# Starting the V projection with the second tile, centred and not yet scaled

## The chip, the cores and the metric

The kernel runs on one core of a Trainium2 chip. The metric is the device time of one execution in microseconds (us). The engines are named as in the profile: PE (TensorE, matmuls), PEld (its weight loads), DVE (VectorE), ACT (ScalarE), POOL (GpSimd) and SP (SyncE, which only issues DMAs here).

## The reference, cut to what matters

There are 2048 tokens of width 576. The input is layer-normalised once, and attention and a gated feed-forward layer are added to it:

```python
xn = _layernorm(x, axis=-1)                 # (x - mean) / sqrt(var + 1e-5)
return x + _A_ref(xn, A_wqkv, A_wo) + _B_ref(xn, B_w1, B_w3, B_w2)

# A: 32 heads of width 18, a causal window of 256 tokens
qkv = (x @ wqkv).reshape(B, S, 3, H, Dh)
scores = einsum("bhqd,bhkd->bhqk", q, k) * (Dh ** -0.5)
p = softmax(where(mask, scores, -1e9))
o = einsum("bhqk,bhkd->bhqd", p, v) @ wo
# B: feed-forward width 4608
h = silu(xn @ w1) * (xn @ w3);  out = h @ w2
```

All inputs are bf16. What matters here is that a row of V is linear in the normalised row of x. The factor 1/sqrt(var + eps) belongs to a token, so it may be applied to the row of V after the matmul just as well as to the row of x ahead of it.

## The kernel before

The tokens are worked on in four chunks of 512 (`CH`), a chunk in four tiles of 128 tokens. A chunk goes through q, k and v projections, then 36 units of the feed-forward layer with attention steps dealt in between, then the second products. The change is in the **prologue**, the first 13 us or so, in which the four tiles of chunk 0 are loaded, normalised, transposed and projected to V before the q and k jobs start. Only chunk 0 has such a prologue; later chunks are prepared beside other work.

The program is written as one list of operations (`add(engine, fn, r=, w=, j=)`). Each engine carries out its own operations strictly in the order of the list; `resolve` turns the reads and writes of named buffers into semaphore waits between engines. So an operation that waits holds up all that is behind it on its engine.

A tile t of the prologue takes these steps:
- The load of x (L304; `xp`), and on POOL a copy that doubles the last 64 columns (L963), so that the 576 columns become 640, five blocks of 128.
- Mean and variance. DVE does this in three operations for tiles 0, 2 and 3 (`ln_stats`: L394 twice, L397). For tile 1 ACT does it in two passes with a running sum (`ln_stats_act`): a Copy with scale -1/D (L385), whose sum is minus the mean, and a Square with that as its bias (L388).
- The root on ACT (`ln_sqrt`, L367), the reciprocal on DVE (L372) and the normalising pass on DVE (`ln_apply`, L411), which writes `xn[t % 2]`.
- The transposes on PE (`xn_turn`, L426): ten of 64 columns for a tile, in pairs on the two halves of the array, into two PSUM banks or two pairs of them; then two moves out of PSUM into `xnT` (L439), on ACT, or one on ACT and one on DVE.
- V on PE (`proj_part`, L491): a first part of 8 matmuls and a second of 10, with 64 rows and 288 columns each. `proj_begin` issues a job's first part and then ends the job that is pending; `proj_end` only ends the pending one. Four moves per tile (`v_evac`, two on ACT L540, two on DVE L542) bring V into `va`.

Some filler matmuls (`warm`, `warm_halves`, L902 and L908) stand in the waits ahead of V. The moves of V can be held back in lists (`moves`, `late`) and put into the program later, so that they don't stand ahead of the next tile's transposes on ACT and DVE.

`xnT` has two slots, one for the chunk at work and one for the next chunk. In the prologue slot 1 is empty. The q and k jobs (L491 with 512 columns) read all four tiles of slot 0, and weights `wp` that POOL copies into order (`deal_...`, L946) as soon as the loads of wqk land. `xn_swap` (L454) sends slot 0 with its halves exchanged to `xnS`, which the feed-forward units (L759) read from their fifth matmul pair on. SP's queue issues, in this order: wv, wqk, the first feed-forward weights (`load_w13`, L328, which wait for the tile named in `behind`), then `xn_swap`.

PSUM has eight banks: three job pairs, `JOBS`, of which `job()` takes one after the other, and the pair `SC`, which the transposes use and V of the last tile.

Of the kernel before, what the change touches and what calls it, by code (L numbers as in the profile page):

```python
# [5 lines left out]
dt = mybir.dt  # L6
# [158 lines left out]
def bass_parallel_sum__sliding_block__glu_gated_swiglu__prompt_kernel(  # L165
# [32 lines left out]
    with ExitStack() as es:  # L198

        def sb(name, shape, dtype=dt.bfloat16):  # L200
            return es.enter_context(nc.sbuf_tensor(name, shape, dtype))
# [12 lines left out]
        eps = sb("eps", [128, 1], dt.float32)  # L214
        sd = [sb(f"sd{i}", [128, 1], dt.float32) for i in range(2)]
        xnT = sb("xnT", [128, 2, 5, CH])
        xnS = sb("xnS", [128, 4, CH])
# [162 lines left out]

        def ln_stats_act(t, s, between):
# [3 lines left out]
            add("act", lambda e: e.activation(junk, xp[s][:, 0:D], ACT.Copy, scale=-1.0 / D, accum_out=vpe[i][:]),  # L385
                r=[("xp", s)], w=[("vpe", i), *keys])
            between()
            add("act", lambda e: e.activation(junk, xp[s][:, 0:D], ACT.Square, bias=vpe[i][:], scale=1.0, accum_out=mv[i][:, 1:2]),  # L388
                r=[("xp", s), ("vpe", i)], w=[("mv", i), *keys])
# [24 lines left out]

        def xn_turn(t, pairs, eng, between=(), by_rows=False):
            i = t % 2
            c, tt = divmod(t, TB)
            ranges = ((0, 2), (2, 5))
            for n, (k0, k1) in enumerate(ranges):
                for k in range(k0, k1):  # L420
                    for r in range(2):
                        r0 = 64 * r
                        b = pairs[n][r]
                        bv = half_bank(b)[:, 64 * k:64 * k + 64]
                        new = k == k0 and (n == 0 or pairs[0] != pairs[1])
                        add("pe", lambda e, bv=bv, r0=r0, k=k: e.transpose(  # L426
                            bv, xn[i][r0:r0 + 64, k * 128:(k + 1) * 128], ident[r0:r0 + 64, r0:r0 + 64],
                            tile_position=(r0, 0)),
                            r=[("xn" if k < 4 else "xnd", i), "ident"], **{"w" if new else "j": [("ps", b)]})
            for what in between:  # L430
                what()
            dst = xnT[:, c % 2, :, tt * 128:(tt + 1) * 128].rearrange("p k (r f) -> p k r f", f=64)
            for n, (k0, k1) in enumerate(ranges):
                b = pairs[n][0]
# [4 lines left out]
                move = (lambda e, d=d, s=s: e.tensor_copy(d, s)) if eng[n] == "dve" else (lambda e, d=d, s=s: e.activation(d, s, ACT.Copy))  # L439
                add(eng[n], move, r=[("ps", b) for b in pairs[n]],  # L440
                    **({"j": [("xnT", c % 2, tt), ("xnTb", tt)] + [("xnTa", tt)] * by_rows} if n else
                       {"w": [("xnT", c % 2, tt), ("xnTa", tt), ("xnTb", tt)]}))

# [22 lines left out]
        def proj_part(c, what, banks, part, behind=()):  # L466

            kind, i = what
            last = []
            early = kind == "v" and c == 0  # L470
            order = range(4 + part if kind == "v" else 5 - part)
            for n in order:
                for r in range(2):
# [4 lines left out]
                    if kind == "q":  # L478
                        t = pair_of(c, i)[x]
                        st, mv = wp[rows, kd, t, :], xnT[rows, c % 2, kd, :]  # L480
                        keys = [("wpd" if n == 4 else "wp", t)] + xk(c)
                    elif kind == "8":
                        out_ = PS[:, banks[x], 0:CH // 2]
                        st, mv = wp[rows, kd, i, :], xnT[rows, c % 2, kd, x * (CH // 2):(x + 1) * (CH // 2)]
                        keys = [("wpd" if n == 4 else "wp", i)] + xk(c)
                    else:
                        out_ = PS[:, banks[x], 0:HD]
                        st, mv = xnT[rows, c % 2, kd, i * 128:(i + 1) * 128], wv[rows, kd, x * HD:(x + 1) * HD]
                        keys = ["wvd" if kd == 4 else "wv", (("xnTb" if kd // 2 else "xnTa"), i) if early and kd < 4 else ("xnT", c % 2, i)]
                    first = part == 0 and n == 0  # L490
# [43 lines left out]
        def v_evac(c, tt, b, r, eng, p):  # L534
# [3 lines left out]
            kw = {"j" if p else "w": [("va", pos)]}  # L538
            if eng == "act":
                add("act", lambda e, dst=dst, src=src: e.activation(dst, src, ACT.Copy), r=[("ps", b), ("ps", b + 1)], **kw)  # L540
            else:
                add("dve", lambda e, dst=dst, src=src: e.tensor_copy(dst, src), r=[("ps", b), ("ps", b + 1)], **kw)  # L542
# [413 lines left out]
        def deal_last(h, d, lo, hi):  # L956
            s0 = lo - (lo > SPREAD)
            deal(h, d, [8], lambda o: o[:, :, 8, s0 * Dh // 2:(s0 + hi - lo) * Dh // 2].rearrange("p k (g c) -> p k g c", c=Dh // 2),
                 lambda i: i[:, :, 1, lo:hi, 3 * Dh // 2:2 * Dh])

        for t in range(TB):
            end = xp[xslot[t]][:, 512:640].bitcast(dt.float32)
            add("pool", lambda e, end=end: e.tensor_copy(end[:, 32:64], end[:, 0:32]), r=[("xp", xslot[t])], w=[("xpd", xslot[t])])  # L963

        moves, late = [], []
# [349 lines left out]
```

## Time and profile before

| what | us |
|---|---|
| median of three runs | 554.58 |
| the three runs | 554.48, 554.58, 555.00 |
| the profiled execution, its own time | 554.48 |
| its span from first to last instruction | 552.7 |
| mean granted TensorE clock | 1.00 |

In a row of the timeline the first number is the start and the second the length, both in us from the start of the span; then come the engine, the line of the kernel, the operation, the tiles written and read, the shapes and a count. Brackets tell how long the engine had been idle and what ended that. A row with a count joins several neighbours. In a row of an answer by line the three numbers are the shortest, median and longest duration in ns. In a row of groups they are the total in us and the mean in ns.

### The profile page before, as it was taken

What the parts mean: (1) busy time and instruction counts of PE and PEld (TensorE: products, weight loads), DVE (VectorE), ACT (ScalarE), POOL (GpSimd) and SP (SyncE); (2) the same over time, 40 slices, a digit from 0 to 9 for tenths busy, and PEclk for the clock granted to TensorE, in tenths of its full rate; (3) what the DMA queues carried; (4) which work ended last, traced back from release to release, by engine and by line L of the source; (5) the groups of instructions that cost most, each with busy time, mean ns of one, the idle gap of its engine ahead of it and who ended that gap; (6) DMA issues with size and microseconds to landing.
All of it is one profiled execution on the core that took longest, in us unless ns stands there. A gap on an engine that the chain in (4) does not pass through costs nothing.

```text
span 552.7 us, 18355 instructions
## 1 busy us (share of the span) xinstructions
PE 548.7 (99%) x8071; PEld 338.7 (61%) x8071; DVE 313.7 (57%) x584; ACT 258.8 (47%) x360; POOL 212.3 (38%) x388
## 2 busy tenths in 40 slices
PE   8999999999999999999999999999999999999998
PEld 5555544777555544577765554559886555445776
DVE  8466797710468886651056988665105567866311
ACT  6456776000288567700047857760005784775000
POOL 6324675400047465530005656643001553663100
PEclk9999999999999999999999999999999999999999
DMA  9997899676577953758646875466763673541750
GB/s 253 209 199 167 197 221 202 138 200 182 141 144 145 177 135 102 176 143 208 182 111 140 172 146 146 112 155 167 194 179 87 138 173 102 152 110 52 195 152 23
DMA packets 128038, 86.00 MB, mean 156 GB/s; under 512 B 35702, under 2 KB 125646, under 8 KB 127958
## 3 DMA queue, kind: packets, MB, share of 16 engines
q1 hardware_dynamic: 89138, 62.80, 49.7%
q10 hardware_dynamic: 38820, 22.02, 15.7%
q8 instruction: 63, 1.03, 0.8%
q14 instruction: 17, 0.14, 0.1%
HBM read 71.29 MB, written 2.36 MB: 133 GB/s over the span
## 4 chain that ended last, share of the span: by engine, by line
PE 98%; DMA 1%; ACT 0%; DVE 0%; issue 0%
PE ps L759 51%; PE ps L832 29%; PE ps L491 10%; PE ps L621 6%; PE ps L689 3%; DMA xp<-in_A_x_dram 1%; DVE stats L394 0%; ACT hT L388 0%; ACT sd L367 0%; PE ps L426 0%; ACT xnT L439 0%; DVE ofin L854 0%; DVE mv L397 0%
## 5 line engine op out<-in xcount | busy, mean ns | idle before, releaser
L759 PE MATMUL ps<-xnT,w 64*128 64x512 bf16 x1400 | 185.3, 376 | 0.0
L759 PE MATMUL ps<-xnS,w 64*128 64x512 bf16 x1120 | 150.6, 376 | 0.0
L832 PE MATMUL ps<-w,hT 64*128 64x288 bf16 x2292 | 144.0, 282 | 0.0
L774 DVE SCALAR_TENSOR_TENSOR gs<-th,ps 128x512 bf16<-128x512 bf16 x144 | 97.9, 680 | 77.7 <-ACT th L768 77.2
L832 PEld LDWEIGHTS ps<-w,hT 64*128 64x128 bf16 x2292 | 117.1, 94 | 24.8 <-issue 0.2
L768 ACT ACTIVATE th<-ps 128x512 bf16<-128x512 f32 x144 | 85.7, 595 | 60.5 <-PE ps L759 59.3
L759 PEld LDWEIGHTS ps<-xnT,w 64*128 64x128 bf16 x1400 | 66.8, 94 | 63.7
L777 DVE SCALAR_TENSOR_TENSOR hT<-gs,ps 128x512 bf16<-128x512 bf16 x144 | 98.9, 687 | 5.0
L658 POOL TENSOR_TENSOR pt<-pt,mk 128x256 bf16<-128x256 bf16 (+1 forms) x143 | 85.6, 622 | 26.3 <-ACT pt L630 26.3
L630 ACT ACTIVATE pt<-ps 128x1024 bf16<-128x1024 f32 (+1 forms) x80 | 80.7, 1009 | 24.0 <-PE ps L621 23.3
L658 POOL TENSOR_TENSOR hT<-hT,mk 128x256 bf16<-128x256 bf16 (+1 forms) x52 | 30.3, 604 | 160.4 <-ACT hT L630 160.4
L759 PEld LDWEIGHTS ps<-xnS,w 64*128 64x128 bf16 x1120 | 53.6, 94 | 51.0
L504 ACT ACTIVATE stage<-ps 128x512 bf16<-128x512 f32 x16 | 9.6, 597 | 139.2 <-PE ps L491 139.2
L863 DVE TENSOR_TENSOR ofin<-ps,xp 128x288 bf16<-128x288 f32 x31 | 12.2, 451 | 98.2 <-PE ps L832 98.2
L621 PE MATMUL ps<-qv,kv 64*128 64x320 bf16 (+4 forms) x528 | 51.4, 260 | 0.0
L621 PEld LDWEIGHTS ps<-qv,kv 64*128 64x128 bf16 x528 | 26.2, 94 | 27.7 <-ACT pt L630 0.8
L491 PE MATMUL ps<-xnT,wp 64*128 64x512 bf16 (+1 forms) x360 | 38.4, 355 | 0.0
L722 DVE STREAM_TRANSPOSE od<-oq 128x256 bf16<-128x256 bf16 x64 | 25.4, 426 | 12.1 <-POOL oq L715 12.1
L630 ACT ACTIVATE hT<-ps 128x1024 bf16<-128x1024 f32 (+1 forms) x28 | 28.4, 1014 | 7.8 <-PE ps L621 7.6
L658 POOL TENSOR_TENSOR stage<-stage,mk 128x256 bf16<-128x256 bf16 (+1 forms) x44 | 24.9, 587 | 14.4 <-ACT stage L630 14.4
L630 ACT ACTIVATE stage<-ps 128x1024 bf16<-128x1024 f32 (+1 forms) x24 | 24.3, 1014 | 7.9 <-PE ps L621 7.8
L491 PEld LDWEIGHTS ps<-xnT,wp 64*128 64x128 bf16 x360 | 18.4, 94 | 14.3
(92 smaller groups left out, 394.2 us busy)
## 6 DMA issues: line engine op xcount, KB each, us to landing
w<-in_B_w_dram SPq DMA_DIRECT2D x210, 192.0 KB, 4.0
w<-in_B_w_dram ACTq DMA_DIRECT2D x70, 288.0 KB, 3.6
xp<-in_A_x_dram SPq DMA_DIRECT2D x29, 144.0 KB, 4.1
out_dram<-ofin SPq DMA_DIRECT2D x31, 72.0 KB, 2.0
xnS<-xnT SPq DMA_DIRECT2D x8, 256.0 KB, 5.0
oT<-od SPq DMA_DIRECT2D x56, 36.0 KB
pt<-in_A_wqkv_dram SPq DMA_DIRECT2D x4, 288.0 KB, 5.3
hT<-in_B_w_dram SPq DMA_DIRECT2D x6, 192.0 KB, 7.1
```

The lines of the kernel that those rows point to most:

```text
L491: op = add("pe", lambda e, out_=out_, st=st, mv=mv, n=n, r0=r0, first=first: e.matmul(out_, st, mv, start=first, stop=(part == 1 and n == ...
L621: add("pe", lambda e, r0=r0, out_=out_, kb=kb, q0=q0, nb=nb: e.matmul(out_, kb4[r0:r0 + 64, g, kb + NV - NB, :] if kb < 0 else kv[r0:r0 + ...
L630: add("act", lambda e: e.activation(pt_slot(sl)[:, :, 0:w], PS[:, SC[0]:SC[1] + 1, 0:w], ACT.Exp, scale=scale), r=[("ps", b) for b in SC], ...
L658: add("pool", lambda e, vb=vb, mm=mm: e.tensor_tensor(vb, vb, mm, ALU.mult), r=(key if n == 0 else []) + ["mk"], **{"w" if n == 0 else "j" ...
L689: add("pe", lambda e, p=p, q=q, pr=pr, sl=sl, g=g, pos=pos, q0=q0, nb=nb, col=col, first=first, n=n: e.matmul(PS[32 * q:32 * q + VW, banks ...
L722: add("dve", lambda e: e.transpose(od[i][:, g % 2, c0:c0 + CH // 2], oq[:, c0:c0 + CH // 2]), r=["oq", "oq0"], **{"j" if half or g % 2 els ...
L759: op = add("pe", lambda e, n=n, r0=r0, r=r, k=k, src=src: e.matmul(PS[:, b0 + r, :], wt[r0:r0 + 64, k, fl * 128:(fl + 1) * 128], src, star ...
L768: add("act", lambda e: e.activation(th[i][:], PS[:, bg, :], ACT.Tanh, scale=0.5), r=[("ps", bg)], w=[("th", i)])
L774: add("dve", lambda e: e.scalar_tensor_tensor(out=gs[i][:], in0=th[i][:], scalar=1.0, in1=PS[:, bg, :], op0=ALU.add, op1=ALU.mult), r=[("t ...
L777: add("dve", lambda e: e.scalar_tensor_tensor(out=hT[:, u, :], in0=gs[i][:], scalar=0.5, in1=PS[:, bu, :], op0=ALU.mult, op1=ALU.mult), r= ...
L832: op = add("pe", lambda e: e.matmul(PS[:, bank, 0:w], stat, move, start=new, stop=False, skip_group_check=True, **tile), r=keys, after=hel ...
L863: add("dve", lambda e: e.tensor_tensor(ofin[:, o, :], PS[:, bank, 0:HD], xp[xs[n]][:, d0:d0 + HD], ALU.add), r=[("ps", bank), ("xp", xs[n] ...
```

## The change

The second tile (tile 1, the one whose statistics ACT makes) becomes the first one that V is made of. Step by step:
- `centre`: one added pass on DVE adds minus the mean to tile 1 and writes `xn[1]`, without the scale. It stands ahead of tile 0's reciprocal.
- Tile 1 is transposed first, into slot 1 of `xnT` (banks of two job pairs), then tile 0 into slot 0 (both halves in `SC`). ACT does all four moves, with the root of tile 2 between tile 0's two moves (`halfway`).
- ACT's Square pass of tile 1 and the statistics' end come only after these moves (`ln_square_act`). Tile 1's root on ACT and its reciprocal and normalising pass on DVE are gone. In their place `root_and_scale` puts three operations on POOL: variance, power -0.5 (`rstd1`), and a 640-column pass that writes the wholly normalised tile 1 into `scaled`, which is a part of `od[0]`. They stand ahead of the `deal` copies.
- V is made in the order tile 1, tile 0, tile 2, tile 3. Tile 1's V is multiplied by `rstd1` on its way out of PSUM (a scale operand on ACT, a `tensor_scalar` on DVE).
- Tile 1 is transposed a second time, from `scaled`, between the two parts of tile 3's V, into slot 0, for the q and k jobs and the feed-forward layer. One move is on ACT, one on DVE.
- Tile 3's root stands ahead of tile 2's move on ACT. All V moves are in lists by tile and put in one by one (`move_v`).
- `proj_end` for tile 3's V comes ahead of the first q job's first part, and `xn_swap` after it in the list.
- The filler pairs are of 256, 128 and 128 columns instead of 256, 256 and 128. `load_w13` waits for tile 0's second move instead of tile 1's.

```diff
+        def centre(s):
+            add("dve", lambda e: e.tensor_scalar(xn[1][:, :], xp[s][:, :], vpe[1][:, 0:1], None, op0=ALU.add),
+                r=[("xp", s), ("xpd", s), ("vpe", 1)], w=[("xn", 1), ("xnd", 1)])
+
+        def root_and_scale(s):
+            add("pool", lambda e: e.tensor_scalar(var1[:], mv[1][:, 1:2], 1.0 / D, 1e-5, op0=ALU.mult, op1=ALU.add),
+                r=[("mv", 1)], w=["var1"])
+            add("pool", lambda e: e.tensor_tensor(rstd1[:], var1[:], neghalf[:], ALU.pow),
+                r=["var1", "neghalf"], w=["rstd1"])
+            add("pool", lambda e: e.tensor_scalar(
+                scaled[:, :], xp[s][:, :], vpe[1][:, 0:1], rstd1[:, 0:1], op0=ALU.add, op1=ALU.mult),
+                r=[("xp", s), ("xpd", s), ("vpe", 1), "rstd1"], w=[("od", 0)])
...
+            if c == 0 and tt == 1:
+                by = rstd1[64 * r:64 * r + 64, 0:1]
+                if eng == "act":
+                    fn = lambda e: e.activation(dst, src, ACT.Copy, scale=by)
+                else:
+                    fn = lambda e: e.tensor_scalar(dst, src, by, None, op0=ALU.mult)
+                add(eng, fn, r=[("ps", b), ("ps", b + 1), "rstd1"], **kw)
...
-        ln_stats_act(1, xslot[1], lambda: ln_sqrt(0))
-        ln_sqrt(1, 1.0 / D)
+        ln_mean_act(1, xslot[1])
+        ln_sqrt(0)
...
+        centre(xslot[1])
         normalise(0)
-        xn_turn(0, (SC, JOBS[1]), ("act", "act"))
-        for cols in (256, 256, 128):
-            warm_halves(JOBS[0], cols)
-        ln_stats(2, xslot[2], 0)
-        ln_stats(2, xslot[2], 1)
-        normalise(1)
-        ln_stats(2, xslot[2], 2)
-        proj_begin(0, ("v", 0))
-        ln_sqrt(2)
-        xn_turn(1, (SC, JOBS[1]), ("act", "act"))
-        load_w13([("xnTb", 1)])
+        xn_turn(1, (JOBS[0], JOBS[1]), ("act", "act"), slot=1)
+        for cols in (256, 128):
+            warm_halves(JOBS[2], cols)
+        for part in range(3):
+            ln_stats(2, xslot[2], part)
+        xn_turn(0, (SC, SC), ("act", "act"), halfway=lambda: ln_sqrt(2))
+        ln_square_act(1, xslot[1])
+        root_and_scale(xslot[1])
+        warm_halves(JOBS[2], 128)
+        proj_begin(0, ("v", 1))
+        load_w13([("xnTb", 0)])
         ln_stats(3, xslot[3], 0)
         normalise(2)
         ln_stats(3, xslot[3], 1)
         ln_stats(3, xslot[3], 2)
-        proj_end(moves, late)
-        proj_begin(0, ("v", 1))
-        ln_sqrt(3)
-        xn_turn(2, (SC, SC), ("act", "dve"), by_rows=True)
+        proj_end(*moves[1])
+        proj_begin(0, ("v", 0))
+        xn_turn(2, (SC, SC), ("act", "dve"), [lambda: ln_sqrt(3)], by_rows=True)
+        proj_end(*moves[0])
         normalise(3)
-        moves.pop(0)()
-        first = [late.pop(0)]
-        proj_end(moves, late)
         proj_begin(0, ("v", 2))
-        xn_turn(3, (SC, SC), ("act", "dve"), first, by_rows=True)
-        for move in moves + late:
-            move()
+        move_v(1, "act")
+        move_v(1, "act")
+        move_v(1, "dve")
+        xn_turn(3, (SC, SC), ("act", "dve"), by_rows=True)
+        move_v(1, "dve")
+        proj_end(*moves[2])
+        proj_begin(0, ("v", 3), SC)
+        move_v(0, "act")
+        move_v(0, "dve")
+        xn_turn(1, (JOBS[2], JOBS[2]), ("act", "dve"), by_rows=True, of=(scaled, ("od", 0), ("od", 0)))
+        for tt in (0, 2):
+            for eng in ("dve", "act"):
+                while moves[tt][eng == "act"]:
+                    move_v(tt, eng)
+        proj_end()
         xn_swap(0, ("sp", "sp"))
-        proj_end()
-        proj_begin(0, ("v", 3), SC)
```

More of the change, by code (lines that the diff above doesn't have):

```diff
@@ L386, in ln_stats_act, with ln_square_act @@
                 r=[("xp", s)], w=[("vpe", i), *keys])
-            between()
+        def ln_square_act(t, s):
+            i = t % 2
+            junk = hT[:, 0:3, :].rearrange("p t c -> p (t c)").bitcast(dt.float32)[:, 0:D]
+            keys = [("h", n) for n in range(3)]
             add("act", lambda e: e.activation(junk, xp[s][:, 0:D], ACT.Square, bias=vpe[i][:], scale=1.0, accum_out=mv[i][:, 1:2]),
@@ L468, in proj_part @@
             kind, i = what
+            vs = 1 if c == 0 and i == 1 else c % 2
             last = []
@@ L487, in proj_part @@
                         out_ = PS[:, banks[x], 0:HD]
[L488 to L489 removed]
+                        st, mv = xnT[rows, vs, kd, i * 128:(i + 1) * 128], wv[rows, kd, x * HD:(x + 1) * HD]
+                        keys = ["wvd" if kd == 4 else "wv", (("xnTb" if kd // 2 else "xnTa"), i) if early and kd < 4 else ("xnT", vs, i)]
                     first = part == 0 and n == 0
@@ L959, in deal_last, with double_end, move_v @@
                  lambda i: i[:, :, 1, lo:hi, 3 * Dh // 2:2 * Dh])
+        scaled = od[0][:, :, :].rearrange("p a q -> p (a q)")[:, 0:640]
+        def double_end(t):
+            end = xp[xslot[t]][:, 512:640].bitcast(dt.float32)
+            add("pool", lambda e: e.tensor_copy(end[:, 32:64], end[:, 0:32]), r=[("xp", xslot[t])], w=[("xpd", xslot[t])])
         for t in range(TB):
-            end = xp[xslot[t]][:, 512:640].bitcast(dt.float32)
-            add("pool", lambda e, end=end: e.tensor_copy(end[:, 32:64], end[:, 0:32]), r=[("xp", xslot[t])], w=[("xpd", xslot[t])])
-        moves, late = [], []
+            double_end(t)
+        moves = [([], []) for _ in range(TB)]
+        def move_v(tt, eng):
+            moves[tt][eng == "act"].pop(0)()
         for p in range(2):
```

21 lines of the change are left out of this document (13 added, 8 removed).

## The prediction

> **What bounds the kernel now.** I read the page's header and busy times first, then the table of windows, then the timeline of the first 13 us engine by engine, then the answers by line for the operations that the change adds.
>
> ```profile
> span 552.7 us, 18355 instructions
> ...
> PE 548.7 (99%) x8071; PEld 338.7 (61%) x8071; DVE 313.7 (57%) x584; ACT 258.8 (47%) x360; POOL 212.3 (38%) x388
> ```
> ```profile
> 6.52:550.30 543.78, 543.78 (x7998) 335.32 (x7998) 308.89 (x573) 254.92 (x352) 208.82 (x374) 1.00 0.66 155
> ```
> The second row is a window; after its length stand the busy times in the order PE, PEld, DVE, ACT, POOL, then clock, DMA share and GB/s. From the first V matmul at 6.52 to 550.30 TensorE is busy for all 543.78 us. So the change can move the time only by the place that TensorE has reached in its list at some point of the prologue; whatever it wins or loses there is carried to the end one for one. Of the 554.48 us of the profiled execution 1.78 lie outside the span and stay. The shown runs have their median at 554.58, 0.10 above it.
>
> I therefore compare one landmark: the start of the second q job (12.93), when all four V tiles and the first half of the first q job are done.
>
> ```profile
> 5.72 0.32 PE L426 MATMUL ps<-ident,xn 64*128 64x64 bf16 x10 [0.56 <-DVE xn L411]
> ...
> 6.52 0.71 PE L491 MATMUL ps<-wv,xnT 64*128 64x288 bf16 x8 [0.21 <-ACT xnT L439]
> ...
> 9.89 0.31 PE L426 MATMUL ps<-ident,xn 64*128 64x64 bf16 x10
> 10.12 1.28 PE L491 MATMUL ps<-wv,xnT 64*128 64x288 bf16 x18
> 11.24 1.25 PE L491 MATMUL ps<-xnT,wp 64*128 64x512 bf16 x10
> ...
> 12.93 1.26 PE L491 MATMUL ps<-xnT,wp 64*128 64x512 bf16 x10
> ```
> Start to start, ten transposes of one tile cost 10.12-9.89 = 0.23. Eighteen V matmuls (one tile: 8 in its first part, 10 in its second) cost 11.24-10.12 = 1.12, which is 0.50 and 0.62. The first half of the first q job and one V second part stand between 11.24 and 12.93, so that half costs 1.69-0.62 = 1.07. From the first V matmul to the landmark: 4 x 1.12 + 3 x 0.23 + 1.07 = 6.24. Before it took 12.93-6.52 = 6.41, so 0.17 is waiting.
>
> **The change, part by part.** After it there are again three sets of transposes behind the first V matmul (third tile, fourth tile, and the second tile once more, scaled), since both first tiles' are now ahead. The same 6.24 is to be done, from another start and with other waits.
>
> *Start.* The rows of ScalarE and VectorE:
>
> ```profile
> 3.77 0.69 ACT L385 ACTIVATE hT<-xp 128x576 f32<-128x576 bf16 x1 [0.21 <-DMA xp<-in_A_x_dram]
> 4.36 0.19 ACT L385 ACTIVATION_READ_ACCUMULATOR hT<-xp 128x1 f32 x1
> 4.69 0.29 ACT L367 ACTIVATE sd<-mv,eps 128x1 f32<-128x1 f32 x1
> 4.89 0.76 ACT L388 ACTIVATE hT<-xp,vpe 128x576 f32<-128x576 bf16 x1
> 5.56 0.19 ACT L388 ACTIVATION_READ_ACCUMULATOR hT<-xp,vpe 128x1 f32 x1
> ...
> 6.00 0.38 ACT L439 ACTIVATE xnT<-ps 128x256 bf16<-128x256 bf16 x1
> ...
> 6.28 0.48 ACT L439 ACTIVATE xnT<-ps 128x384 bf16<-128x384 bf16 x1
> ```
> ```profile
> 5.02 0.16 DVE L372 RECIPROCAL rstd<-sd 128x1 f32<-128x1 f32 x1 [0.36 <-ACT sd L367]
> 5.22 0.45 DVE L411 TENSOR_SCALAR xn<-xp,mv,rstd 128x640 bf16<-128x640 bf16 x1
> 5.58 0.81 DVE L394 BATCH_NORM_STATS2 stats<-xp 128x6 f32<-128x288 bf16 x2
> ```
> A handover costs 0.03 to 0.06 (5.22+0.45 = 5.67, then TensorE at 5.72). The mean of the second tile is there at 4.55; the added centring, of the shape of L411, runs 4.60 to 5.05 in the 0.36 that VectorE idles ahead of its reciprocal, so the first tile's chain (5.02, 5.22, transposes at 5.72) does not move. The second tile's transposes start at 5.10, their two moves on ScalarE at 5.38 and 5.66 (0.28 behind, 0.28 apart, as 5.72, 6.00 and 6.28), done at 5.76 and 6.14. The weights then decide:
>
> ```profile
> L894 SPq DMA_DIRECT2D wv<-in_A_wqkv_dram x2: 581/582/582, 1.7 to 2.3; - x2
> L890 SPq DMA_DIRECT2D wv<-in_A_wqkv_dram x1: 418/418/418, 1.3 to 1.3; - x1
> ...
> DMA to landing us min/median/max: 4.5/4.7/4.7
> ```
> L890 is issued at 1.3 and lands 4.5 to 4.7 later, 5.8 to 6.0; V starts at 6.03 instead of 6.52, 0.49 sooner. Its last slice (2.3 + 4.7 = 7.0 at most) is wanted at 7.03. The filler matmuls taken out (three pairs of sizes 256, 256, 128 become 256, 128, 128) stood in waits and cost nothing either way. V of the second tile: 6.03 to 7.15.
>
> *ScalarE's new order.* The first tile's moves both need all ten transposes, since they share one bank pair; the distance for that is 0.35 (9.89 to 10.24 below).
>
> ```profile
> 7.98 0.45 DVE L394 BATCH_NORM_STATS2 stats<-xp 128x6 f32<-128x288 bf16 x1
> 8.47 0.21 DVE L397 BATCH_NORM_AGGREGATE mv<-stats 128x2 f32<-128x12 f32 x1
> ```
> ```profile
> 8.71 0.30 ACT L367 ACTIVATE sd<-mv,eps 128x1 f32<-128x1 f32 x1 [0.61 <-DVE mv L397]
> 8.91 0.42 ACT L439 ACTIVATE xnT<-ps 128x320 bf16<-128x320 bf16 x1
> ...
> 10.24 0.44 ACT L439 ACTIVATE xnT<-ps 128x320 bf16<-128x320 bf16 x1 [0.62 <-PE ps L426]
> ```
> First move 6.07. The third tile's statistics end at 6.39, its aggregate at 6.64, and the root that stands between the two moves runs at 6.67; the second move starts 0.20 behind it (8.71 to 8.91), 6.87 to 7.35. That just serves V of the first tile, 7.15 to 7.65 for its first part. Behind it Square takes 7.25 to 8.01, its sum is read 7.92 to 8.11. The third tile is normalised 7.20 to 7.65 (root out at 6.97, reciprocal 7.00), transposed 7.70 to 7.93 (0.05 lost), and V of the first tile ends at 8.55.
>
> *First new wait.* The fourth tile's second statistics stand behind that normalisation: 7.56 to 8.02, aggregate 8.05 to 8.26, root at 8.29. The third tile's move on ScalarE is queued behind that root though its data are there at 8.05: 8.49 to 8.91. V of the third tile starts at 8.97 instead of 8.55: 0.42 lost. Before, the same start was 9.89-0.50 = 9.39. So the earlier start itself is worth nothing beyond this point; what counts is that this chain is 0.42 sooner.
>
> *Second new wait.* The scale of the second tile, on GpSimd:
>
> ```profile
> L376 POOL TENSOR_SCALAR vpe<-mv x12: 221/221/222, 71.2 to 317.4; 128x1 f32<-128x1 f32 x12
> ```
> ```profile
> L378 POOL TENSOR_TENSOR rstd<-vpe,neghalf x12: 567/567/572, 71.5 to 317.7; 128x1 f32<-128x1 f32 x12
> ```
> ```profile
> L540 ACT ACTIVATE va<-ps 64x288 bf16<-64x288 f32 x32 | 12.8, 401 | 4.5 <-PE ps L491 4.1
> ```
> Sum at 8.11, variance 8.15, power 0.30 behind it (71.2 to 71.5), 8.45 to 9.02. Two V moves of the second tile stand on ScalarE ahead of the fourth tile's move and wait for it until 9.05. One costs 0.40 by L540; the scale operand is not in a row of that shape, so bounds: nothing, or the 0.08 by which L388 with an operand exceeds L385 without; I take 0.08, the like instruction. [...] Moves 9.05 to 9.53 and 9.54 to 10.02. The fourth tile, transposed 9.47 to 9.70, could move at 9.82 and moves at 10.03 to 10.46. V of the third tile ends 10.32, V of the fourth starts 10.51: 0.19 lost.
>
> *Second transposes.* They go into the banks of the second tile's V, the last of which VectorE empties behind its half of the fourth tile's move:
>
> ```profile
> 10.24 0.32 DVE L439 COPY xnT<-ps 128x320 bf16<-128x320 bf16 x1
> 10.59 0.46 DVE L542 CAST va<-ps 64x288 bf16<-64x288 f32 x1
> ```
> That move comes at 9.82 here, the emptying 0.35 later, 10.17 to 10.63. The scaled tile is there sooner (below). So: first part of the fourth tile's V 10.51 to 11.01, transposes to 11.24, their moves 11.36 to 11.80, beside the second part of V, 11.24 to 11.86. That cover leaves nothing: the first q job wants the moves at 11.86.
>
> Landmark: 6.03 + 6.24 + 0.05 + 0.42 + 0.19 = 12.93. Before: 12.93. The gain of 0.49 and the 0.17 of old waits are paid out as 0.66 of new ones.
>
> *GpSimd.* Its added 640-column pass starts at 9.05; it stands ahead of the copies that make the q and k weights.
>
> ```profile
> 8.82 1.01 POOL L946 COPY wp<-pt 128x288 f32<-128x288 f32 x3 [2.09 <-DMA pt<-in_A_wqkv_dram]
> 10.06 3.40 POOL L946 COPY wp<-pt 128x288 f32<-128x288 f32 x11 [0.23 <-DMA pt<-in_A_wqkv_dram]
> ```
> ```profile
> L658 POOL TENSOR_TENSOR pt<-pt,mk 128x256 bf16<-128x256 bf16 x115 | 75.1, 670 | 26.3 <-ACT pt L630 26.3
> ...
> L946 POOL COPY wp<-pt 128x576 f32<-128x576 f32 x1 | 0.7, 666 | 0.0
> ```
> Bounds for the pass: 0.67 x 640/576 = 0.74 by the one-input copy, 0.67 x 640/256 = 1.68 by the two-input product. I take 0.74, one tensor input. The copies then start at 9.79 instead of 8.82, and all fourteen (1.01 + 3.40) end at 14.20. The first q job needs three of them (10.80 against 11.86). The third q job needs all, at 12.93 + 1.07 + 0.86 (eight matmuls, 4/5 of 1.07) = 14.86: 0.66 to spare. At 1.68 they end at 15.14, 0.3 late. [...]
>
> *Queues.* The loads of w13 on SP's queue wait for the first tile's second move, 7.35 instead of 8.13, and queue behind the same loads as before; the half swap (xnS) stands behind them:
>
> ```profile
> 8.13 4.85 SPq L328 DMA_DIRECT2D w<-in_B_w_dram x6
> ```
> ```profile
> L454 SPq DMA_DIRECT2D xnS<-xnT x2: 537/566/596, 13.1 to 13.7; - x2
> ...
> DMA to landing us min/median/max: 6.2/6.5/6.9
> ```
> ```profile
> 21.47 1.04 PE L759 MATMUL ps<-xnS,w 64*128 64x512 bf16 x8
> ```
> Its data are ready at 11.80, ahead of the 13.1 at which it was issued; it lands by 13.7 + 6.9 = 20.6 and is used at 21.47. Nothing lost, 0.9 in hand.
>
> **The rivals.** *A, the new waits don't come* (faster). If ScalarE reached the third and fourth tiles' moves as soon as their transposes are done, 0.61 is saved: 554.58-0.61 = 553.97; if only the second wait goes, 554.39. For it: those data are ready at 8.05 and 9.82. Against: ScalarE takes its list in order, and the root and the power are measured rows. *B, the weights' copies come late* (slower). Place: GpSimd's pass; it decides from 14.82 (14.86 less a handover) - 4.41 = 10.41, a pass over 1.36. At 1.68, and held up by one VectorE pass of 0.45, it ends at 11.18, the third q job is 0.77 late, and the time is 555.35. Against: one tensor input; for: a data type and scalars that no row of GpSimd joins at this width. [...] *C, V begins no earlier* (the change doesn't do what it says): wv lands late, by up to 0.5. The third tile's V is set by the root's chain at 8.97, so the time stays at 554.6.
>
> **How the numbers follow.** Forecast 554.58 + 0.00 = 554.6: 0.66; C, with the same time: 0.06; A 0.14; B 0.14. Range 554.0 (A) to 555.3 (B). A measurement of this kernel can tell about 0.2% (1.1 us) from no change. All of A lies within it; 0.03 for faster covers what the rows don't show. B passes it only from a pass of 1.36 + 1.1 = 2.5 us, 3.8 ns a column against 2.6 in the dearest row; 0.07 for slower. Within: 0.90.
>
> **What would show it.** Right: V from about 6.0; on ScalarE the fourth tile's root ahead of the third tile's move, and V of the third tile near 9.0, not 8.6; two waits of 0.2 to 0.4 in TensorE's starts; the second q job near 12.9; weights' copies from about 9.8, and no wait of TensorE on GpSimd. Wrong: the second q job before 12.5 (A) or after 13.3, or a third q job that waits for L946's copies (B); any new wait behind 21 us; a granted clock below 1.00.

## The result and the profile after

The changed kernel takes 556.08 us in the median (555.44 to 557.45, 11 runs) against 554.73 (554.48 to 555.64, 11 runs) of the kernel before on the same chip: ratio 1.0024, 95% interval 1.0017 to 1.0032. It is 1.35 us slower, where no change was forecast and the range ended at 555.3. The profiled execution took 556.08 as well, with a span of 554.3 against 552.7. So the two traces can be compared directly: there are 1.6 us to find.

The page of the changed kernel, header and busy times:

```profile
span 554.3 us, 18378 instructions
...
PE 550.4 (99%) x8081; PEld 338.9 (61%) x8081; DVE 314.4 (57%) x584; ACT 259.0 (47%) x360; POOL 213.9 (39%) x391
```

TensorE is as full as before and runs ten more matmuls (the second tile's second transposes). Its timeline over the prologue:

```profile
0.83 4.43 PE L944 MATMUL ps<-const-bfloat16-1.0 128*128 128x512 bf16 x55 [0.83 <-PEq L1347]
5.07 0.72 PE L932 MATMUL ps<-oq 128*128 128x512 bf16 x2
5.72 0.45 PE L446 MATMUL ps<-ident,xn 64*128 64x64 bf16 x10
...
6.28 0.48 PE L446 MATMUL ps<-ident,xn 64*128 64x64 bf16 x10
6.57 0.26 PE L938 MATMUL ps<-oq 64*128 64x128 bf16 x2
6.65 2.00 PE L514 MATMUL ps<-wv,xnT 64*128 64x288 bf16 x26
...
9.79 0.66 PE L514 MATMUL ps<-wv,xnT 64*128 64x288 bf16 x8 [0.29 <-ACT xnT L462]
10.63 0.32 PE L446 MATMUL ps<-ident,xn 64*128 64x64 bf16 x10 [0.17 <-DVE xn L417]
10.78 1.49 PE L514 MATMUL ps<-wv,xnT 64*128 64x288 bf16 x18
12.16 0.32 PE L446 MATMUL ps<-ident,od 64*128 64x64 bf16 x10
...
13.06 1.47 PE L514 MATMUL ps<-xnT,wp 64*128 64x512 bf16 x12
...
21.81 0.40 PE L789 MATMUL ps<-xnT,w 64*128 64x512 bf16 x2
```

V begins at 6.65, V of the third tile at 9.79, the q jobs at 13.06 and so the second one at 14.13 (1.07 behind), and the first feed-forward unit at 21.81. Before, that unit began here:

```profile
20.61 1.04 PE L759 MATMUL ps<-xnT,w 64*128 64x512 bf16 x8
```

So 1.20 of the 1.6 us are lost in the prologue. Nearly all of the rest (0.36) is lost in the middle of the kernel, at a single place, inside a pair of matmuls that nothing in the trace holds up (after, then before):

```profile
239.34 0.28 PE L862 MATMUL ps<-wo,oT 64*128 64x288 bf16 x1
239.80 0.28 PE L862 MATMUL ps<-wo,oT 64*128 64x288 bf16 x1 [0.18 <-issue]
```
```profile
238.13 0.29 PE L832 MATMUL ps<-wo,oT 64*128 64x288 bf16 x2
```

The pair ran joined before, and here its halves start 0.46 apart. From there on the changed kernel is 1.6 us behind. What released the prologue's waits is seen on the other engines:

```profile
7.08 0.28 ACT L369 ACTIVATE sd<-mv,eps 128x1 f32<-128x1 f32 x1
...
8.58 0.19 POOL L426 TENSOR_SCALAR varv<-mv 128x1 f32<-128x1 f32 x1 [1.90 <-ACT hT L394]
...
8.88 0.21 DVE L403 BATCH_NORM_AGGREGATE mv<-stats 128x2 f32<-128x12 f32 x1 [0.47 <-POOL varv L426]
...
9.12 0.29 ACT L369 ACTIVATE sd<-mv,eps 128x1 f32<-128x1 f32 x1 [0.62 <-DVE mv L403]
9.32 0.41 ACT L462 ACTIVATE xnT<-ps 128x320 bf16<-128x320 bf16 x1
...
9.52 0.87 POOL L430 TENSOR_SCALAR od<-xp,vpe,rstdv 128x640 bf16<-128x640 bf16 x1
9.64 0.99 ACT L565 ACTIVATE va<-ps,rstdv 64x288 bf16<-64x288 f32 x2
9.65 0.92 DVE L417 TENSOR_SCALAR xn<-xp,mv,rstd 128x640 bf16<-128x640 bf16 x1
```

VectorE's aggregate of the fourth tile waits 0.47 for GpSimd's variance of the second. It isn't data that it waits for; both use `mv[1]`. The second tile's sum of squares lies there until GpSimd has read it, and the aggregate of the fourth tile (same parity) overwrites it. Before, the root on ScalarE read it long before. Behind the late aggregate stands the root (9.12), which is ahead of the third tile's move on ScalarE (9.32); and the fourth tile's normalising pass now falls beside GpSimd's 640-column pass and takes 0.92 instead of 0.45.

### The profile page after: what moved, and what is told of

Its sections match the earlier page's. It is cut to its first block, busy times and chain, and to the rows that moved or that the text cites. A ratio compares the mean times of both kernels' runs of the same rounds, so it can differ in the third digit from the quotient of the medians.

```text
span 554.3 us, 18378 instructions
## 1 busy us (share of the span) xinstructions
PE 550.4 (99%) x8081; PEld 338.9 (61%) x8081; DVE 314.4 (57%) x584; ACT 259.0 (47%) x360; POOL 213.9 (39%) x391
## 3 DMA queue, kind: packets, MB, share of 16 engines
q1 hardware_dynamic: 89138, 62.80, 44.8%
## 4 chain that ended last, share of the span: by engine, by line
PE 99%; ACT 0%; DVE 0%; issue 0%; POOL 0%; DVEq 0%
PE ps L789 51%; PE ps L862 29%; PE ps L514 9%; PE ps L651 6%; PE ps L719 3%; PE ps L944 1%; ACT xnT L462 0%; DVE xn L417 0%; PE ps L446 0%; ACT hT L394 0%; PE ps L932 0%; ACT sd L369 0%; DVE ofin L884 0%; DVE mv L403 0%; POOL varv L426 0%
## 5 line engine op out<-in xcount | busy, mean ns | idle before, releaser
L862 PEld LDWEIGHTS ps<-w,hT 64*128 64x128 bf16 x2292 | 115.9, 94 | 26.3 <-issue 0.7
```

The lines of the kernel that those rows point to most:

```text
L862: op = add("pe", lambda e: e.matmul(PS[:, bank, 0:w], stat, move, start=new, stop=False, skip_group_check=True, **tile), r=keys, after=hel ...
```

## The experiments

Every kernel was timed in five rounds, in three groups of four, each group on one chip beside the kernel before (554.66, 554.64 and 554.66). Behind a median stand in brackets the fastest and the slowest run, then the ratio to the kernel before and its 95% interval; there are 11 runs where no number is given. "Shift" is TensorE's lag behind the profiled kernel before, at equal work.

**1. A tile of its own for the sum of squares.**

```diff
+        msq1 = sb("msqv", [128, 1], dt.float32)
-... accum_out=mv[i][:, 1:2]), ... w=[("mv", i), *keys])
+... accum_out=msq1[:]), ... w=["msq1", *keys])
```

> The changed kernel, but the sum of squares of the second tile goes into a tile of its own instead of mv[1], which the fourth tile's aggregate overwrites. Theory 1 (hidden wait): in the changed kernel the fourth tile's aggregate idles 0.47 us for GpSimd's read of mv[1]; here it follows its statistics at once (idle under 0.05), the fourth tile's root, the third tile's move and V of the third tile come 0.3 to 0.5 sooner, and the normalising pass of the fourth tile lies mostly ahead of GpSimd's 640-column pass; the second q job starts 0.5 to 0.8 sooner than at 14.13, and the time is about 0.6 us less than the changed kernel's (near 0.13% above before instead of 0.24%). [...] Rival (late clock alone): no change in time beyond the spread, as the start of V decides.

The aggregate no longer waits, and the fourth tile's pass now begins ahead of GpSimd's (9.23) and takes 0.45 again:

```profile
8.15 0.21 DVE L404 BATCH_NORM_AGGREGATE mv<-stats 128x2 f32<-128x12 f32 x1
...
8.93 0.45 DVE L418 TENSOR_SCALAR xn<-xp,mv,rstd 128x640 bf16<-128x640 bf16 x1
```

V of the third tile starts at 9.07, of the fourth at 10.67, the second q job at 13.13: the prediction's steps (8.97, 10.51, 12.93) to 0.2. Of the 1.00 that the second q job gains on the changed kernel, 0.41 is V's earlier start in this run (6.24 instead of 6.65; see "The start" below). But the median is 556.13 (555.14 to 558.35, 8 runs; 1.0028, 1.0015 to 1.0041). The shift is 0.20 at the first unit and 1.58 at the end; about 0.6 of the difference comes at three places that experiment 5 is on, and 0.39 near 501 us, in a pause for which the trace shows no releaser either. So the missed wait is real, and its removal uncovered that the end isn't set by the prologue alone.

**2. GpSimd's pass put behind the fourth tile's pass on VectorE** (`mv[1]` still shared). Theory 2 is that VectorE's pass takes 0.92 in the changed kernel because GpSimd's runs beside it.

```diff
+        def scale_pass(s, behind=()):
...
-                r=[("xp", s), ("xpd", s), ("vpe", 1), "rstd1"], w=[("od", 0)])
+                r=[("xp", s), ("xpd", s), ("vpe", 1), "rstd1", *behind], w=[("od", 0)])
...
         normalise(3)
+        scale_pass(xslot[1], [("xn", 1)])
         proj_begin(0, ("v", 2))
```

> The changed kernel, but GpSimd's 640-column pass stands behind the fourth tile's normalising pass on VectorE and waits for it, so that the two never run together. [...] Rival (VectorE's pass is long for another reason): it still takes about 0.9 and the second q job starts later than at 14.13. Theory 1 expects the fourth tile's aggregate to wait 0.47 as before.

```profile
8.78 0.21 DVE L403 BATCH_NORM_AGGREGATE mv<-stats 128x2 f32<-128x12 f32 x1 [0.47 <-POOL varv L426]
...
9.55 0.45 DVE L417 TENSOR_SCALAR xn<-xp,mv,rstd 128x640 bf16<-128x640 bf16 x1
...
10.18 0.87 POOL L432 TENSOR_SCALAR od<-xp,vpe,rstdv 128x640 bf16<-128x640 bf16 x1 [0.87 <-DVE xn L417]
```

The wait on `mv[1]` is as long as in the changed kernel, but VectorE's pass is back at 0.45. GpSimd's takes 0.87 alone as well. The second q job begins at 13.56 instead of 14.13, and the median is 555.74 (555.28 to 555.98; 1.0018, 1.0009 to 1.0027). So VectorE's pass is lengthened by GpSimd's running beside it (0.92, against 0.45 without it). Which of the two begins first matters: in experiments 1, 7, 11 and 12 VectorE's pass begins 0.22 to 0.31 ahead, overlaps GpSimd's by 0.14 to 0.23 and still takes 0.45.

**3. Twelve of the 64-column opening fillers fewer.**

```diff
-        for k, n in enumerate([CH] * 3 + [128] * 4 + [64] * 48):
+        for k, n in enumerate([CH] * 3 + [128] * 4 + [64] * 36):
```

> The changed kernel with 36 instead of 48 filler matmuls of 64 columns at the start. Theory 3 (late clock): when the full clock is granted only at about 6.6 us, the fillers at half pace (0.053 us each) end at 5.07 and hold the second tile's transposes until 5.72; 12 fewer end 0.64 sooner, the transposes start at about 5.2, V at 6.1 instead of 6.65, and all behind it 0.4 to 0.5 sooner, time about 0.4 us less than the changed kernel's. When the clock is granted at about 3.5 us nothing changes. Rivals: theories 1 and 2 alone leave the second q job where it is, since the waits behind are absolute.

555.26 (555.16 to 557.03; 1.0014, 1.0005 to 1.0023). V starts 0.31 earlier (6.34), the second q job at 13.83; the shift is 0.90 at the first unit and 0.82 at the end. The pause at 239 us is gone. That can't come from 12 fillers' time in the first 5 us, so the count itself came under suspicion.

**4. The three together.**

> The changed kernel with all three edits: own tile for the sum of squares, GpSimd's pass behind the fourth tile's normalising pass, 36 fillers. If the three theories hold the loss: the second q job starts at about 12.9 to 13.2, as in the kernel before, and the time is within 0.3 us of before. If the loss comes from elsewhere (weights' copies late, or a stall in the middle of the kernel): still 0.8 us or more slower than before, with the second q job near its old place.

555.53 (554.80 to 556.67; 1.0015, 1.0006 to 1.0024). The profiled run had a span of 553.1, the second q job at 13.11 as expected, a shift of 0.18 at the first unit and 0.32 at the end, but half of the runs took over 555.5. Something else spreads them; experiments 7 to 11 are on that.

**5. The kernel before with ten more opening fillers of the same columns** (55 become 65; the changed kernel's count, 8081).

```diff
-        for k, n in enumerate([CH] * 3 + [128] * 4 + [64] * 48):
+        for k, n in enumerate([CH] + [128] * 8 + [64] * 56):
```

> The kernel before, with its 55 opening filler matmuls cut into 65 of the same columns in all (one of 512, eight of 128, 56 of 64), so that TensorE's list is 10 matmuls longer, as long as the changed kernel's (8081), at the same filler time. Theory I (where instruction fetches fall): the stretches of TensorE in the middle of the kernel in which it waits for nothing but its instructions move with the count of instructions ahead; with 8081 a stall of 0.3 to 0.5 us shows at the same matmul as in the changed kernel (the second of a pair on wo and oT near 238.5 us) and the time is 0.4 to 0.8 us above before. Rival P (the prologue alone): the time is that of before within 0.2 us.

555.50 (554.59 to 555.64; 1.0011, 1.0003 to 1.0020), 0.86 above before, with no part of the change in it. Its prologue is on time, and it pauses where the changed kernel does:

```profile
20.55 1.04 PE L759 MATMUL ps<-xnT,w 64*128 64x512 bf16 x8
```
```profile
238.58 2.87 PE L832 MATMUL ps<-w,hT 64*128 64x288 bf16 x44 [0.18 <-issue]
```

Counted over all of TensorE's instructions in the trace (matmuls, weight loads and those of its sequencer, 16234 in the kernel before), the one behind this pause is number 6851, in the changed kernel 6849, in experiments 1 and 2 the same. It is other work in the kernel before than in the changed one, but the same place in TensorE's list. The other such pauses of all the traces (0.14 to 1.21 from start to start instead of 0.12) stand at 2754 or 2755, 10945 to 10947 and 15041 or 15042: 4096 instructions apart. The 14 traces have 56 such places and 12 pauses at them: three each in experiments 1, 2 and 5, one in the changed kernel, two in experiment 8 (the only one without the ten extra matmuls that has any), none in the kernel before. In this experiment's trace the three take about 0.8 of the 1.02 us by which it ends late. The queue q8 brings instructions in 63 packets of 16 KB, some 256 to a packet if they are TensorE's 16234. At the 12 pauses the last packet had landed 1.25 to 1.52 us before the matmul that came late. At the 44 places without a pause it had landed 1.31 to 2.41 before, in 35 of them more than 1.52. So a packet that landed late goes with every pause, but nine places had one as late and no pause. Two pauses without a releaser stand elsewhere: 0.22 us at 501.12 in experiment 1, 0.24 us at 83.94 in experiment 8.

**6. The changed kernel with ten opening fillers fewer, same columns** (45; 8071 as before).

```diff
-        for k, n in enumerate([CH] * 3 + [128] * 4 + [64] * 48):
+        for k, n in enumerate([CH] * 3 + [128] * 14 + [64] * 28):
```

> The changed kernel, with its 55 opening filler matmuls joined into 45 of the same columns in all, so that TensorE's list has the length of the kernel before (8071). Theory I: the stall near 239.6 us is gone, the shift against before stays what the prologue makes it (about 1.2 us with a late clock, less with an early one), and the time is about 0.4 us less than the changed kernel's, 0.8 above before. Rival P: the time is the changed kernel's, 1.35 above before.

555.38 (555.15 to 555.69; 1.0014, 1.0005 to 1.0023). The wait and the long pass are still there, V of the third tile starts at 9.32 and the second q job at 13.66. The shift is 0.73 at the first unit and 0.69 at the end. What the prologue loses is now passed on one for one, 0.74 in the median. The other 0.61 of the changed kernel's 1.35 went with the ten matmuls. The intervals of the two kernels overlap, so the size is rough.

**7. Experiments 1 and 6 together.**

> The changed kernel with both: the sum of squares of the second tile in a tile of its own, and 45 fillers of the same columns (8071 matmuls). Theory 1 and theory I together: the second q job starts at about 13.1, the shift against before is 0.2 at the first feed-forward unit and stays so to the end within 0.2, time 0.2 to 0.4 us above before. Rival (stalls in the middle come at random, whatever the count): shift of 0.2 at the first unit, but 0.5 to 1.4 at the end, time as that of the kernel with an own tile alone, 1.4 above before.

The profiled run took 554.51, with the second q job at 13.01 and a shift of 0.03 at the end, as the sum says. But the median is 555.41 (554.51 to 557.11; 1.0016, 1.0004 to 1.0028). Against experiment 1 it is again the ten matmuls alone that are fewer: 0.77 above before instead of 1.47. The four kernels with the added tile in this place (1, 4, 7, 8) share the wide spread. The pages show one more thing that these share, the time of the weights' queue (kernel 7, then kernel 6):

```profile
q1 hardware_dynamic: 89138, 62.80, 51.3%
```
```profile
q1 hardware_dynamic: 89138, 62.80, 44.7%
```

Packets and bytes are the same. The added 4-byte tile stands ahead of all large ones and moves them by 32 bytes. The changed kernel's two new ones had moved them by 64 (queue share 49.7% before, 44.8% after).

**8. Both ScalarE queue waits moved away** (own tile; the fourth tile's root behind the third tile's move, one of the second tile's V moves behind the fourth tile's move, 45 fillers).

```diff
-        xn_turn(2, (SC, SC), ("act", "dve"), [lambda: ln_sqrt(3)], by_rows=True)
+        xn_turn(2, (SC, SC), ("act", "dve"), by_rows=True, halfway=lambda: ln_sqrt(3))
-        move_v(1, "act")
         move_v(1, "dve")
         xn_turn(3, (SC, SC), ("act", "dve"), by_rows=True)
+        move_v(1, "act")
```

> The changed kernel with an own tile for the sum of squares; the fourth tile's root behind the third tile's move on ScalarE instead of ahead of it; one of the two V moves of the second tile behind the fourth tile's move instead of ahead; 45 fillers with 12 x 64 columns fewer (8071 matmuls). If the two waits that the prediction named stand in ScalarE's order: V of the third tile starts without a wait (about 8.8 at an early clock), V of the fourth without one, the second q job at about 12.6 to 12.8, and the time is 0.1 to 0.3 us below before. If they don't: the second q job at 13.1 as with the own tile alone.

A miss: 555.63 (555.37 to 558.67, 12 runs; 1.0028, 1.0017 to 1.0040). The wait ahead of the third tile's V did go (it starts at 9.06, straight behind the matmuls before it). But with the root behind the move (and V 0.44 later than in experiment 11, below, after 0.25 of waiting for the load of `wv`) the fourth tile's pass comes later, so that it begins behind GpSimd's again:

```profile
9.36 0.87 POOL L431 TENSOR_SCALAR od<-xp,vpe,rstdv 128x640 bf16<-128x640 bf16 x1
9.41 1.01 DVE L418 TENSOR_SCALAR xn<-xp,mv,rstd 128x640 bf16<-128x640 bf16 x1
```

The second q job begins at 13.98. The large tiles lie as in experiment 7, so this time doesn't tell the new order from their place. The profiled run is the longest one. Behind 21 us TensorE waits 1.3 for weights in it, and 0.9 is one of the pauses of experiment 5 (the columns are total, times, longest):

```profile
PE ps L790 <- DMA w<-in_B_w_dram: 1.3, 1, 1.3
PE ps L863 <- issue: 0.9, 1, 0.9
```

**9 and 10. The kernel before with two, and with three, unused 4-byte tiles** ahead of `xnT`. Its order and instructions are those of before.

```diff
+        pad = [sb(f"pad{i}", [128, 1], dt.float32) for i in range(2)]    # 9; range(3) in 10
         xnT = sb("xnT", [128, 2, 5, CH])
```

> The kernel before with two unused 4-byte tiles ahead of xnT, so that every larger tile lies where the changed kernel has it, 64 bytes further than before. Order and instructions are those of before. If the place of the tiles sets what the transfers take: the weights' queue q1 falls from 49.7% to about 45% of the span (the changed kernel 44.8%). If the share comes from the changed order: it stays at 49.7%. Time: 554.6 either way (554.4 to 554.9) if transfers are hidden; a gain of 0.3 us or more would say that a part of the time of before is waiting on transfers. Second q job at 12.9.

> The kernel before with three unused 4-byte tiles ahead of xnT: the places of the three kernels with a sum-of-squares tile of their own (96 bytes further than before). If the place of the tiles sets what the transfers take: q1 at about 51% (those kernels 50.9 to 51.9%). If later transfers are also what spreads their times: runs spread over 1.5 us or more, as there (555.1 to 558.4 for the first of them), with a median 0.3 to 1.0 us above before. If the spread is the changed order's own: runs within 0.6 us of each other, and 554.6.

Two tiles: 554.57 (554.34 to 554.76; 0.9997, 0.9988 to 1.0005). Three: 555.64 (554.40 to 557.07; 1.0020, 1.0010 to 1.0029). Their queues, and the transfers of w13 (median from issue to landing):

```profile
q1 hardware_dynamic: 89138, 62.80, 45.5%
...
w<-in_B_w_dram SPq DMA_DIRECT2D x210, 192.0 KB, 3.9
```
```profile
q1 hardware_dynamic: 89138, 62.80, 51.8%
...
w<-in_B_w_dram SPq DMA_DIRECT2D x210, 192.0 KB, 4.3
```

The place of the tiles alone moves the queue share both ways, as far as in the changed kernels. 45% instead of 50% gains nothing that can be measured; at 52% the runs spread over 2.7 us and the median rises by 0.98. In the profiled run with three tiles, 0.46 late at the end, the loss stands in the prologue: the third tile's statistics wait 0.48 for their load of x, and the second q job begins at 13.43. What its slower runs lose, no trace shows.

**11. Experiment 7 with the added tile behind all others**, so that the large ones lie as in the changed kernel.

```diff
-        msq1 = sb("msqv", [128, 1], dt.float32)
...
         ofin = sb("ofin", [128, NOF, HD])
+        msq1 = sb("msqv", [128, 1], dt.float32)
```

> The changed kernel with a sum-of-squares tile of its own and 45 fillers, as in own_minus10, but the tile stands behind all others, so that the larger tiles lie as in the changed kernel. If the place of the tiles matters: q1 at about 45%, the runs within 0.6 us of each other, and a median of 554.5 to 554.9 (the profiled landmark 13.0, the time of before plus 0.1). If it doesn't: as own_minus10, 555.4 with runs from 554.5 to 557.1.

554.67 (554.49 to 555.00; 1.0000, 0.9992 to 1.0009), the queue at 45.3%. Its prologue:

```profile
4.99 0.32 PE L447 MATMUL ps<-ident,xn 64*128 64x64 bf16 x10
...
5.93 1.02 PE L515 MATMUL ps<-wv,xnT 64*128 64x288 bf16 x10
```
```profile
8.91 0.36 PEld L515 LDWEIGHTS ps<-wv,xnT 64*128 64x128 bf16 x8 [0.43 <-ACT xnT L463]
8.99 1.00 ACT L566 ACTIVATE va<-ps,rstdv 64x288 bf16<-64x288 f32 x2
9.07 0.89 POOL L431 TENSOR_SCALAR od<-xp,vpe,rstdv 128x640 bf16<-128x640 bf16 x1
...
10.50 0.36 PEld L515 LDWEIGHTS ps<-wv,xnT 64*128 64x128 bf16 x8 [0.38 <-ACT xnT L463]
```

This is the change as its order intends it, without the shared buffer and at the old number of matmuls: no faster and no slower than before. Against experiment 6, which differs in the shared buffer alone, it is 0.71 less in the median and 0.69 less at the second q job (12.97 against 13.66). The first feed-forward unit (experiment 6, then 11):

```profile
21.34 1.02 PE L789 MATMUL ps<-xnT,w 64*128 64x512 bf16 x7
```
```profile
20.64 1.04 PE L790 MATMUL ps<-xnT,w 64*128 64x512 bf16 x8
```

**12. And one of the second tile's two V moves on ScalarE behind the fourth tile's move.**

```diff
-        move_v(1, "act")
         move_v(1, "dve")
         xn_turn(3, (SC, SC), ("act", "dve"), by_rows=True)
+        move_v(1, "act")
```

> As own_tail_minus10, and one of ScalarE's two scaled V moves of the second tile goes behind the fourth tile's move. The fourth tile's V begins 0.2 to 0.3 us earlier (10.54 in own_minus10, so 10.25 to 10.35), the second q job 0.1 to 0.25 earlier than in own_tail_minus10 (12.75 to 12.9). If the landmark is passed on: 0.1 to 0.25 us below own_tail_minus10, thus at or up to 0.2 us below before. If what follows the prologue sets the end: no difference to own_tail_minus10.

554.70 (554.32 to 554.85; 0.9999, 0.9991 to 1.0008): no gain over experiment 11 that can be measured. From V's start to the second q job its profiled run needs 6.66 (6.66 to 13.32) instead of 7.04. Only a part of the 0.38 is the edit's: the wait ahead of the fourth tile's V fell from 0.24 to 0.07. A wait of 0.29 ahead of the third tile's V went too, but the edit doesn't touch it: in that run V itself began 0.73 later, for the reason told next. What the median run keeps, these runs don't show. No version beats the kernel before.

## Why the prediction was wrong

**The sum.** Of the 1.35 us, 0.73 is the shared buffer with its sequel (experiment 6 against 11) and 0.61 went with the ten matmuls (the changed kernel against 6), each time against its own before. Neither was in the prediction. What was in it came out at 0.01 (experiment 11), as forecast. The split is rough, since each ratio has an interval of half a microsecond either way; the ten matmuls are worth 0.70 between experiments 1 and 7, and 0.86 in experiment 5. The profiled runs of the changed kernel and of 6 differ by 0.92 at the end, of which 0.47 is a later start (below) and the rest came in the middle.

**The step that failed first: "First new wait".** It let the fourth tile's aggregate run at 8.05, behind its statistics on VectorE. I followed the data and each engine's order, but not the buffers: every tile of the same parity shares `mv`, and the change moves the last reader of `mv[1]` from ScalarE to GpSimd and behind Square. The wait takes 0.47 on VectorE, and V of the third tile starts at 9.79 instead of 8.97. About half of these 0.82 us is the wait, a term that the sum had at nothing. The other half is that the third tile's root ran at 7.08, not 6.67 (below).

**The pass on GpSimd**, taken at 0.74, took 0.87 to 0.97, inside its bounds of 0.74 to 1.68. The weights' copies hold up no job (the third q job follows the second after 1.08, as before), so rival B's place was wrong. What I missed is that the pass lengthens VectorE's: 0.92 against 0.45 (experiment 2). Rival B's sum holds GpSimd's pass up by one VectorE pass of 0.45, a term that no run shows: GpSimd's took 0.87 alone (experiment 2) and 0.87 to 0.97 beside VectorE's. One row of before came near: the fourth tile's pass took 0.49 beside GpSimd's weight copies, where the others took 0.45.

**The start.** V was to begin at 6.03 and began at 6.65. The prediction let the second tile's transposes wait for the centring alone, and left out the opening fillers, which stand ahead of them in TensorE's list. The centring ended at 4.92 (4.53 + 0.39), but the 55 opening fillers took 4.43 instead of 3.78, and L932 0.72 instead of 0.45, so that TensorE reached the transposes at 5.72. In experiment 11, with the same columns in 3.91, they started at 4.99 and V at 5.93: the 5.10 and 6.03 of the prediction. It is the clock that varies from run to run, not the number of fillers: experiments 11 and 12 have the same opening, and it took 3.91 and 4.43. The record of the full clock begins at 3.51 us in the profiled run of before, 6.65 in that of the changed kernel, 3.83 in experiment 11 and 6.72 in 12; ahead of it 64-column fillers start 0.053 apart, behind it 0.032. Over the twelve traces with such a record its beginning spreads over 3.2 us; what sets it, no trace shows. When the clock came in the runs that were not profiled is not known. Before, it didn't matter:

```profile
0.83 4.43 PE L914 MATMUL ps<-const-bfloat16-1.0 128*128 128x512 bf16 x65 [0.83 <-PEq L1300]
...
6.54 0.42 PE L491 MATMUL ps<-wv,xnT 64*128 64x288 bf16 x4 [0.21 <-ACT xnT L439]
```

This is experiment 5, the old order with slow fillers, and V starts at 6.54, as with fast ones (6.52), because there TensorE waited for the first tile's normalisation until 5.72 in any case. The earlier start made TensorE's own opening the last to arrive, in a run with the late clock. Rival C (V begins no earlier) came true in this run, but for another reason, and its price of nothing was wrong: with the transposes, the third tile's root moved by 0.41 too.

**"Carried to the end one for one"** held in experiments 6 and 11 (0.73 to 0.69, 0.03 to 0.10) and failed for the changed kernel, where 1.20 became 1.6. The premise rested on TensorE's having no wait behind 21 us in one trace. In the changed kernel's trace nothing there waits for another engine or a load either, but pauses with no releaser come and go with the number of TensorE's instructions. That the ten matmuls bring them is shown in both directions (experiments 5 and 6, and 7 against 1), and so is where most of them stand: at every 4096th instruction, each time with the last packet of instructions landed no more than 1.52 us before. This speaks for a late delivery of instructions, but doesn't show it, since nine packets as late brought no pause. Why ten matmuls bring these places nearer to their packets, no run shows.

**Right** were ScalarE's order and the second new wait (V of the fourth tile at 10.50 in experiment 11, predicted 10.51), the scaled move (1.00 for two, thus 0.50, against 0.48), the landmark without the shared buffer (12.97 against 12.93, though V began 0.10 sooner there and took 7.04 to it instead of 6.90), and that rival A's gains don't come. The sign to watch was named too: the second q job after 13.3 and a new wait behind 21 us, both of which appeared.

## What to carry to other kernels

When a step is moved to another engine or later in the list, list its buffers as well as its data: for each one that it reads, find who writes it next, and put that writer's wait into the sum. A difference of a microsecond in a kernel whose TensorE is 99% busy can come from the number of instructions (0.61 to 0.86 us for ten matmuls here) or from where the tiles lie (0.98 us for three unused tiles of 4 bytes); a control with the old order and the new count, and one with the old order and the new places, tells these from the change. Starting an engine's work earlier makes whatever stands ahead of it, fillers included, part of the critical path: in the changed kernel fillers held the first transposes until 5.72 us, though their data were there at 4.92.

## What was not expected of the hardware

- Ten more matmuls at the start, of the same columns in all, cost 0.86 us in the median, mostly as pauses 200 us and more later, at places 4096 instructions of TensorE apart, where the last packet of instructions had landed 1.34 to 1.48 us before (experiment 5).
- Unused tiles of 4 bytes ahead of the large ones change the time of the transfers: the weights' queue is busy for 49.7% of the span with none, 45.5% with two and 51.8% with three, with the same packets. In the built programs the first weights tile (`w13_0`) starts at byte 65728 of a partition with none, 65792 with two and 65824 with three. Why the share goes with the place, no run shows. The lower share gained nothing that can be measured (554.57 against 554.66). In the five kernels at 51 to 52% the runs spread by 1.9 to 3.3 us, in the other changed or padded ones by 0.4 to 2.0; but the kernel before, at 49.7%, spread by 0.8 to 3.1 in its groups of 11 to 35 runs, so the spread alone proves little.
- VectorE's 640-column pass takes 0.92 to 1.01 us when GpSimd's pass of the same width began 0.05 to 0.13 ahead of it, against 0.45 alone, and ends 0.18 behind GpSimd's in all four such traces. When it began first itself (four traces), it took 0.45, and GpSimd's 0.89 to 0.97, ending 0.75 behind. The fixed distances look as if one pass waits for the other, rather than both going slower.
